# Attention, a dense layer and top-2 experts on one core: masks, maxima and weight norms computed by other engines, the order up to the first expert made anew, and the scatters of one expert left without an order

## The chip, the cores and the metric

The kernel runs on one core of one Trainium2 chip. A core has TensorE (PE, with its weight loads shown apart as PEld), VectorE (DVE), ScalarE (ACT), GpSimd (POOL) and SyncE (SP, which only issues transfers), and 16 DMA engines. The metric is the device time of one execution in microseconds, median of 3 runs.

## The reference

Three stages follow one another on 2304 tokens (4 batches of 576) of 512 values:

```python
# attention, 8 heads of 64, scale 1/8, twice
out_d     = sm_attn(mean4(q), mean4(k), mean4(v))          # 144 groups of 4 positions, repeated 4 times
scores    = where(|pos_i - pos_j| < 4, scale * q @ k.T, -1e9)
x         = repeat(out_d, 4) + softmax(scores) @ v
# dense layer, 512 -> 2048 -> 512
x         = relu(x @ w_in)**2 @ w_out
# 8 experts, 512 -> 1024 -> 512, each token goes to its best two
noisy     = x @ w_gate + log1p(exp(x @ w_noise)) * noise
top2, wts = best two of noisy, softmax over them
out[tok] += wts[tok, k] * (relu(x[tok] @ w1[e]) @ w2[e])   # for e in 0..7, k in 0..1
```

`w_in` and `w_out` come as 64-bit floats; the kernel turns their bits into 32-bit floats on the chip.

## The kernel before

**How it is tiled.** A float32 operand of a large product is scaled by a power of two and split into a high and a low float16 half (`wih`, `wil`; `gh`, `gl`), and each product is three float16 matmuls. The power of two comes from a norm, so nothing of `w_in` can be split before all of `w_in` has been read and converted. Attention is cut into 32 units (4 batches, 4 pairs of heads, 2 parts of the sequence). The dense layer goes over 9 chunks of 256 tokens, each in 8 steps of 256 hidden columns. The experts follow one after another, 5 tiles of 128 slots (the last of 112) each.

**What sets the order.** Up to the end of expert 0 the program is a list of tokens, `ORDER`, written out ahead: each token is one small function with an index, and each engine runs its instructions in the order of that list. Attention of unit u is `S` (local scores, L263), `D` (pooled scores, L277), `ml`/`md` (maxima, L286 to L299), `el`/`ed` (exponentials, ACT), `nl`/`nd` (sums and division, the division of batch 0 by POOL), `PT` (transposes and their evictions), `PW` (product with v) and `xb` (split of the result). `vg`, `vm`, `vs` load v, square it for its maximum, and sum groups of four. `Xa`, `Xb` make the scale of a batch. A piece of `w_in` goes through `il ia ib ic ij` (load; ACT, DVE, ACT, DVE convert it), `is` (ACT squares it, L960) and `in` (PE sums the squares of columns, L966); then `wS` makes the scale and `wh`/`wl` split the weights (ACT L982, DVE L989). `w_out` goes through `ol oa oB oc oj`, `os` (ACT squares and sums, L1011), `of` (scale), `oh`/`oo` (split). `M` is the first product of the dense layer (L577), `r` its activation (L585, L589, and the float16 copy `gh` by DVE, L599), `yh`/`yl` and `Y` the second product (L643, L619). Tokens from `ga` on are the gate and the rows written out for the experts; `pe`, `cm`, `cw` prepare and run expert 0.

**The start.** POOL builds the identity, a triangle and the masks with `affine_select` (L123 to L144); the mask scratch shares a buffer (`tag="jv"`) with the squares of v. DVE clears the buffers `pTs` and `vws`. The maximum over partitions is `partition_all_reduce` on POOL (L213 for x, L975 for `w_in`).

**The experts 1 to 7** are a plain loop (L1133). Turn e first calls `load_rows(e + 1)`: two transfers on SP and then four small DVE instructions, which make the row weights `om` and the row numbers `tk` (L857 to L862). Then come 16 steps of `c_m1` (12 matmuls, L873, then ACT L875 and DVE L876) between which the next expert's weights are split, then `load_e`, then 5 steps of `c_m2` (24 matmuls L887, DVE scales the result into `ob`, L889, POOL starts a scatter with addition to `out`, L890). Both `tk` and `om` have two buffers, `ob` has three. All scatters write the tensor `out`, so each waits until the one before it has landed.

Of the kernel before, what the change touches and what calls it, by code (L numbers as in the profile page):

```python
# [62 lines left out]
yh18 oo7 vw7 xb5 PW6 yh13 yh21 SD0 yl11 el8 pz0 yh26 yl21 el7 yh27 nl8 yl16 D9 S10 qk7 nl7 vg5 yh1 r6 yl25 yl19
yl8 yl29 nd7 r4 vm5 yl1 yl3 M7 G6 yl27 yl10 r7 yh16 yh30 yh20 xb6 PT7 yh8 D10 yl22 vs5 nd8 yh6 yh29 yh7 PW7 yh23
md9 pg0 yh31 ml9 yh28 PT8 yl20 yh25 ml10 el9 xb7 vw8 yh14 yl24 pf0 pf1 yl14 nl9 yl12 yl23 md10 vg6 ed9 M9 vm6
pf2 vs6 S11 PW8 r9 G7 yl18 pf3 nd9 vw9 M10 vw10 ed10 M13 yh24 D11 vg7 ip0 r10 el10 PT9 yl2 M12 vm7 md11 yh15 yl7
yl28 nl10 ml11 vs7 el11 nd10 yl31 ed11 Xa1 S13 r13 Xb1 pf4 pf5 xb8 vg8 D13 PT10 S12 D12 pf6 md13 M8 nl11 yl26
nd11 ed13 ml12 yl6 md12 yh19 PW9 vw11 r12 pf7 el12 PT11 yl30 zo0 ml13 xb9 yh4 r8 nl12 M11 PW10 r11 ed12 el13 M15
xb10 yh22 S14 nd12 S15 yl4 nl13 PW11 r15 xb11 M14 yl15 yh12 nd13 r14 PT12 D14 md14 ga1 M16 ml14 gb1 vm8 PT13
el14 ed14 D15 ga0 qk8 nl14 ml15 M17 el15 Y8 vw12 Y9 ip1 vs8 Y10 Y11 S16 qk9 nd14 gb0 md15 r16 vw13 r17 PW12 gc0  # L70
M19 ed15 G8 xb12 vg9 nl15 PW13 S17 gd0 nd15 Y12 PT14 vm9 Y13 ml16 gc1 gf0 gd1 M18 PT15 Y14 gf1 qk10 vs9 ge0 r19
Y15 ge1 D16 md16 M23 G9 r18 M22 gg1 gg0 ed16 vg10 vw14 xb13 D17 el16 r23 PW14 r22 M21 ga2 vm10 nl16 S18 md17 ga3
# [19 lines left out]
r67 Z2 ge15 gg15 r71 M69 r69 pe12 M70 r70 Y67 Y68 pe13 Y69 Y70 Y71 pe14 Z3 pe15 ga16 Z4 Z5 gb16 Z6 pe16 Z7 ga17  # L92
lr0 gc16 gb17 cm6 gd16 gc17 le1 gf16 gd17 cm7 pe17 ge16 pe18 gf17 gg16 cm0 cm3 cm1 pe19 pe20 ge17 pe21 gg17 cm2
cm4 pe22 cm5 pe23 pe24 cw1 pe25 pe26 pe27 cw0 lr1 pe28 cw2 cm15 pe29 cm10 cm9 pe30 cm11 cm8 pe31 cm14 pe32 cm13
cm12 pe33 lr2 le2 cw4 cw3
"""


@with_exitstack
def moe_kernel(ctx, tc, qk_in, vwin, vgrp, w_in, w_out, w_gate, w_noise, noise, w1, w2, out):  # L100
# [45 lines left out]
    for t in pms:  # L146
        nc.gpsimd.memset(t, 0.0)
# [1115 lines left out]
```

## Time and profile before

| | us |
|---|---|
| median of 3 runs (lowest, highest) | 1012.27 (1011.76, 1012.81) |
| the profiled execution, own time | 1015.63 |
| its span, first to last instruction | 1013.6 |
| PE, DVE, ACT, POOL busy | 921.0, 602.1, 484.9, 131.4 |
| mean granted clock of TensorE | 0.977 of full speed |

Busy times are those of the profiled execution and are a share of its span; a time left idle on PE is the span less 921.0, or 92.6 us. Rows of the trace give the start of an instruction or of a merged run of like instructions, its length, the engine, the source line, what it writes and reads, and in square brackets how long the engine had been idle and what it had waited for.

### The profile page before, as it was taken

What the parts mean: (1) busy time and instruction counts of PE and PEld (TensorE: products, weight loads), DVE (VectorE), ACT (ScalarE), POOL (GpSimd) and SP (SyncE); (2) the same over time, 40 slices, a digit from 0 to 9 for tenths busy, and PEclk for the clock granted to TensorE, in tenths of its full rate; (3) what the DMA queues carried; (4) which work ended last, traced back from release to release, by engine and by line L of the source; (5) the groups of instructions that cost most, each with busy time, mean ns of one, the idle gap of its engine ahead of it and who ended that gap; (6) DMA issues with size and microseconds to landing.
All of it is one profiled execution on the core that took longest, in us unless ns stands there. A gap on an engine that the chain in (4) does not pass through costs nothing. (4 is left out here: it accounts for less than half of the span.)

```text
span 1013.6 us, 20138 instructions
## 1 busy us (share of the span) xinstructions
PE 921.0 (91%) x8159; PEld 614.6 (61%) x8159; DVE 602.1 (59%) x1833; ACT 484.9 (48%) x1043; POOL 131.4 (13%) x171
## 2 busy tenths in 40 slices
PE   2538999999999999999999998999999899989992
PEld 1426888666676667666666464656565647455651
DVE  5899977678868776857677562525161616153220
ACT  4899956445544345343544544627162525341100
POOL 2312000010101000101011111020201020111111
PEclk9999899999999999999999898999999899999997
DMA  9743588533333111116124577637365463721212
GB/s 317 251 160 108 162 306 306 143 118 54 73 91 109 45 38 54 51 30 220 22 64 112 198 172 192 186 41 215 53 186 74 113 145 103 157 29 21 31 22 33
DMA packets 104184, 121.70 MB, mean 120 GB/s; under 512 B 69264, under 2 KB 69264, under 8 KB 102032
## 3 DMA queue, kind: packets, MB, share of 16 engines
q1 hardware_dynamic: 95568, 100.57, 34.1%
q0 software_dynamic: 8512, 19.74, 10.2%
q8 instruction: 66, 1.08, 0.4%
q14 instruction: 38, 0.31, 0.1%
HBM read 70.33 MB, written 35.28 MB: 104 GB/s over the span
## 5 line engine op out<-in xcount | busy, mean ns | idle before, releaser
L577 PE MATMUL ph<-xall,wih 128*128 128x256 f16 x1152 | 197.6, 278 | 3.9 <-ACT wih L982 3.8
L873 PEld LDWEIGHTS <-we 128*128 128x128 f16 x1536 | 153.3, 100 | 71.2 <-issue 20.9
L887 PE MATMUL po<-we,h 128*128 128x512 f16 (+1 forms) x840 | 182.4, 379 | 0.0
L873 PE MATMUL phc<-xT,we 128*128 128x384 f16 (+1 forms) x1152 | 158.2, 300 | 9.7 <-DVE h L876 9.7
L577 PE MATMUL ph<-xall,wil 128*128 128x256 f16 x576 | 159.6, 277 | 2.7 <-DVE wil L989 2.6
L887 PEld LDWEIGHTS <-h 128*128 128x128 f16 (+1 forms) x840 | 87.6, 104 | 92.3
L875 ACT ACTIVATE h<-phc 128x384 f16<-128x384 f32 (+1 forms) x112 | 47.6, 428 | 179.5 <-PE phc L873 161.6
L619 PE MATMUL y<-wo,gh 128*128 128x512 f16 x448 | 133.3, 379 | 0.0
L577 PEld LDWEIGHTS <-wih 128*128 128x128 f16 x1152 | 111.9, 100 | 22.1 <-ACT wih L982 3.9
L889 DVE TENSOR_SCALAR ob<-po,om 128x512 f32<-128x512 f32 (+1 forms) x35 | 26.3, 751 | 148.8 <-PE po L887 148.8
L890 POOL DMA_INDIRECT out_dram<-ob,tk x35 | 53.8, 1538 | 326.9 <-DVE ob L889 203.3
L619 PE MATMUL y<-wo,gl 128*128 128x512 f16 x224 | 84.9, 379 | 0.0
L876 DVE SCALAR_TENSOR_TENSOR h<-phc,h 128x384 f16<-128x384 f32 (+1 forms) x112 | 52.2, 479 | 50.2 <-ACT h L875 49.4
L780 POOL DMA_INDIRECT xs<-row,si x36 | 36.9, 1026 | 338.5 <-issue 133.5
L619 PEld LDWEIGHTS <-gh 128*128 128x128 f16 x448 | 42.1, 98 | 44.7 <-issue 0.4
L577 PEld LDWEIGHTS <-wil 128*128 128x128 f16 x576 | 57.3, 100 | 10.9 <-DVE wil L989 3.1
L585 ACT ACTIVATE r<-ph 128x512 f32<-128x512 f32 x72 | 42.3, 587 | 19.8 <-PE ph L577 19.0
L589 ACT ACTIVATE g<-r 128x512 f32<-128x512 f32 x72 | 45.4, 630 | 2.3
L602 DVE TENSOR_TENSOR gl<-g,gh 128x512 f16<-128x512 f32 x64 | 44.5, 696 | 2.3
L825 ACT ACTIVATE we<-w1raw,sce 128x1024 f16<-128x1024 f32 x32 | 35.2, 1139 | 18.5 <-DVE sce L158 15.2
L599 DVE CAST gh<-g 128x512 f16<-128x512 f32 x64 | 27.1, 423 | 26.2 <-ACT g L589 25.3
L826 DVE SCALAR_TENSOR_TENSOR we<-w1raw,sce,we 128x1024 f16<-128x1024 f32 x32 | 40.4, 1282 | 2.2 <-ACT we L825 1.8
(331 smaller groups left out, 1360.3 us busy)
## 6 DMA issues: line engine op xcount, KB each, us to landing
w1raw<-in_moe_w_dram SPq DMA_DIRECT2D x8, 2048.0 KB
w2raw<-in_moe_w_dram SPq DMA_DIRECT2D x8, 2048.0 KB
xs<-zrow SPq DMA_DIRECT2D x8, 1290.0 KB
qkT<-in_qk_dram SPq DMA_DIRECT2D x16, 579.0 KB
raw<-in_moe_w_out_dram SPq DMA_DIRECT2D x8, 1024.0 KB
out_dram<-zrow SPq DMA_DIRECT2D x1, 4864.0 KB
raw<-in_moe_w_in_dram SPq DMA_DIRECT2D x4, 1024.0 KB
vw<-in_vwin_dram SPq DMA_DIRECT2D x48, 76.0 KB
```

What stands on the lines that cost most here:

```text
L577: nc.tensor.matmul(ph[:, f], a[:, kk, fo], bb[:, kk], start=(n == 0), stop=(n == 11))
L585: nc.scalar.activation(r, ph, AF.Relu, scale=KAPPA)
L589: nc.scalar.activation(g, r, AF.Square)
L602: nc.vector.tensor_tensor(gl, g, gh, op=OP.subtract)
L619: nc.tensor.matmul(py[c, tt], a[:, o], bb[:, ft], start=(ft == 0 and n == 0), stop=(ft == 15 and n == 2))
L780: st = nc.gpsimd.indirect_dma_start(out=xs, out_offset=bass.IndirectOffsetOnAxis(ap=si[:, kk:kk + 1], axis=0), in_=roww, in_offset=None)
L826: nc.vector.scalar_tensor_tensor(wl[:, o], raws[i][:, o], ss[i], wh[:, o], op0=OP.mult, op1=OP.subtract)
L873: nc.tensor.matmul(ph[:, :n], a[:, fo], xT[:, bb], start=(i == 0), stop=(i == 11))
L875: nc.scalar.activation(hh[:, f], ph[:, :n], AF.Relu)
L876: nc.vector.scalar_tensor_tensor(hl[:, f], ph[:, :n], 0.0, hh[:, f], op0=OP.max, op1=OP.subtract)
L887: nc.tensor.matmul(po, a[:, f, jo], bb[:, do], start=(i == 0), stop=(i == 23))
L890: nc.gpsimd.indirect_dma_start(out=out, out_offset=bass.IndirectOffsetOnAxis(ap=tk[:m], axis=0), in_=ob[:m], in_offset=None, compute_op=OP ...
```

## The change

- The identity and the masks are made by DVE with two small matmuls that turn a row of numbers into a column; POOL keeps two memsets and one `affine_select`, for the triangle. The mask scratch has a buffer of its own, and `idh` is made later. ACT runs one exponential of a column first.
- For the units of batch 0 and for part 0 of batch 1 (12 units of 32) one more matmul (`idb` with `masks`) puts the masks into PSUM ahead of the local scores, and the addition by DVE falls away.
- The maximum over partitions is a transpose by PE, a maximum by DVE on one partition, and a matmul that spreads it. A token `Xm`, or `wT` and `wU`, stands for each further step.
- The norm of `w_in`: per piece 8 products of a 128x128 block of its upper 16 bits with itself, collected in four PSUM tiles (`in`), and per half two maxima by DVE (`is`, now two tokens and not eight). The squares by ACT and L966 fall away. The norm of `w_out`: 8 such products and one DVE instruction per piece (`os`), and the squares by ACT (L1011) fall away.
- `r` becomes `ra` in 56 of its 72 steps: the float16 copy is made by ACT, as a second square, and not by DVE.
- In the expert loop the row weights of experts 2 to 7 are made by `row_weights(e)` after the 16 steps of `c_m1` of the same expert. The scatters of one expert are declared independent of each other, except those of expert 0.
- `ORDER` is a new list of the same length.

```diff
 ORDER = """
...
-xb2 PW3 is6 oa1 in4 G4 oB1 in5 S7 in6 is7 ol3 oc0 ol2 in7 ed5 wS0 xb3 qk5 nl5 oc1 wh6 wh7 oj0 wl6 wh0 nd5 vw4 S8
-oa3 oa2 oj1 wh5 wl7 vw5 wh3 wl0 os1 oB2 M0 wl3 wh2 wl5 oB3 oc2 M5 oj2 wl2 os0 oc3 of1 oj3 wh1 wh4 os2 wl4 PW4 D7
...
+ib6 in2 in3 ic5 ml5 ia7 nl4 is3 PW2 ic6 el5 in4 ib7 ij5 vw3 xb2 ij6 ic7 oa3 ed5 in5 ij7 in6 in7 oB3 oa0 oB0 oa2
+is7 nd4 ol1 PW3 wS0 S6 oB2 oc0 oc3 wT0 oj3 oa1 wU0 oc2 vw4 oB1 os3 wh5 oj2 wh1 qk4 S7 wl5 xb3 oc1 vg5 D6 wh4 md6
+PT4 wl1 oj1 os2 wh0 oj0 wh7 wl0 nl5 vw5 wh6 M5 wl6 os1 wh2 wh3 qk5 wl7 M0 D7 wl4 qk6 of3 nd5 wl3 os0 wl2 ed6 r0
...
 """
...
-    idf = const.tile([P, P], F32, name="idf")
-    nc.gpsimd.memset(idf, 0.0)
-    nc.gpsimd.affine_select(idf, idf, [[-1, P]], OP.not_equal, 1.0, base=0, channel_multiplier=1)
...
-    masks = const.tile([P, 9, KW], BF16, name="masks")
-    mask = sp.tile([P, 512], BF16, tag="jv", name="mask", bufs=1)[:, :KW]
-    nc.gpsimd.memset(mask, 0.0)
-    for j in range(4):
-        m = mask[32 * j:32 * j + 32]
-        nc.gpsimd.affine_select(m, m, [[1, KW]], OP.is_ge, NEG, base=0, channel_multiplier=-1)
-        nc.gpsimd.affine_select(m, m, [[-1, KW]], OP.is_ge, NEG, base=6, channel_multiplier=1)
...
     pms = [ap.tile([P, 5, 64], F32, name=f"pm{i}", bufs=1) for i in range(2)]
-    for t in pms:
-        nc.gpsimd.memset(t, 0.0)
...
+    nc.gpsimd.memset(onesf, 1.0)
+    nc.gpsimd.memset(pms[0], 0.0)
+
+    pw = pms[1].rearrange("p a b -> p (a b)")
+    it, r32, dc = pw[:, :P], pw[:, P:2 * P], pw[:, 2 * P:2 * P + KW]
+    nc.vector.memset(it[:, 0:1], 0.0)
+    for n in (1, 2, 4, 8, 16):
+        nc.vector.tensor_scalar(it[:, n:2 * n], it[:, :n], float(n), None, op0=OP.add)
+    nc.vector.tensor_copy(r32.rearrange("p (a b) -> p a b", b=32), it[:, None, :32].to_broadcast([P, 4, 32]))
+    for n in (32, 64):
+        nc.vector.tensor_scalar(it[:, n:2 * n], it[:, :n], float(n), None, op0=OP.add)
...
+    nc.tensor.matmul(pc0_[:, 1:2], r32[0:1], onesf[0:1, 0:1], start=True, stop=True)
+    nc.tensor.matmul(pc0_[:, 0:1], it[0:1], onesf[0:1, 0:1], start=True, stop=True)
+    nc.vector.tensor_copy(pidx, pc0_[:, :2])
+    nc.vector.tensor_scalar(dc, it[:, :KW], pidx[:, 1:2], 3.0, op0=OP.subtract, op1=OP.subtract)
+    nc.vector.tensor_tensor(dc, dc, dc, op=OP.mult)
+    nc.vector.tensor_scalar(mask, dc, 9.5, NEG, op0=OP.is_gt, op1=OP.mult)
+    nc.vector.tensor_copy(masks, mask[:, None, :].to_broadcast([P, 9, KW]))
+    for j in (0, 64):
+        nc.vector.memset(masks[j:j + 32, 0, :3], NEG)
+        nc.vector.memset(masks[j + 32:j + 64, 7, KW - 3:], NEG)
+    nc.vector.tensor_scalar(idb, it, pidx[:, 0:1], None, op0=OP.is_equal)
+    nc.vector.tensor_scalar(idf, it, pidx[:, 0:1], None, op0=OP.is_equal)
+    nc.vector.memset(pms[1], 0.0)
     for i in range(2):
         nc.vector.memset(pTs[i][0], 0.0)
         nc.vector.memset(vws[i][32:64], 0.0)
+    nc.vector.tensor_copy(onesb, onesf)
+    nc.gpsimd.affine_select(trib, onesb, [[1, P]], OP.is_gt, 0.0, base=0, channel_multiplier=-1)
+
+    tiny = sp.tile([P, 1], F32, name="tiny", bufs=1)
+    nc.scalar.activation(tiny, onesf[:, :1], AF.Exp)
...
+    XB, GX, MB = 5, 3, 3
...
     def x_scale(b):
         m1 = sp.tile([P, 1], F32, tag="xm", name="xm")
         nc.vector.tensor_reduce(m1, vmx[b], AX.X, OP.max)
+        nc.vector.tensor_scalar(m1, m1, 1.0e-30, None, op0=OP.max)
+        sx[b] = across(m1)
+
+    def across(m1):
+
+        pt = psT.tile([P, 512], F32, tag="tp", name="pmx")
+        nc.tensor.transpose(pt[0:1, :P], m1, idf)
+        return pt
+
+    def across2(pt):
         m2 = sp.tile([P, 1], F32, tag="xm2", name="xm2")
-        nc.vector.tensor_scalar(m1, m1, 1.0e-30, None, op0=OP.max)
-        nc.gpsimd.partition_all_reduce(m2, m1, P, bass.bass_isa.ReduceOp.max)
-        sx[b] = m2
+        nc.vector.tensor_reduce(m2[0:1], pt[0:1, :P], AX.X, OP.max)
+        nc.tensor.matmul(pt[:, P:P + 1], onesf[0:1], m2[0:1], start=True, stop=True)
+
+    def x_scale1(b):
+        across2(sx[b])
 
     def x_scale2(b):
-        m2 = sx[b]
+        pt = sx[b]
         sx[b] = const.tile([P, 1], F32, name=f"sx{b}")
-        pow2_of_sumsq(sx[b], m2, A_X)
+        pow2_of_sumsq(sx[b], pt[:, P:P + 1], A_X)
...
+        pre = 2 * b + part < MB
+        if pre:
+            nc.tensor.matmul(s_[:, :ng * KW], idb, masks[:, 4 * part:4 * part + ng].rearrange("q g c -> q (g c)"),
+                             start=True, stop=False)
...
-                                     qT[o, 32 * t:32 * t + 32], kT[o, 32 * t:32 * t + KW], start=True, stop=True)
+                                     qT[o, 32 * t:32 * t + 32], kT[o, 32 * t:32 * t + KW], start=not pre,
+                                     stop=not pre or i == ng - 1)
...
-        nc.vector.tensor_tensor(pl, s_[:, :ng * KW].rearrange("q (g c) -> q g c", c=KW),
-                                masks[:, 4 * part:4 * part + ng], op=OP.add)
...
+        src = s_[:, :ng * KW].rearrange("q (g c) -> q g c", c=KW)
+        if 2 * b + part >= MB:
+            nc.vector.tensor_tensor(pl, src, masks[:, 4 * part:4 * part + ng], op=OP.add)
+            src = pl
+        nc.vector.tensor_reduce(mx[:, :ng], src, AX.X, OP.max)
...
+        R[e, j0, "mt"] = mt
+        if e < 2:
+            row_weights(e, j0, j1, pool)
+
+    def row_weights(e, j0, j1, pool):
+        n = j1 - j0
+        nb = 1 if pool is sp else 2
+        m = R[e, j0, "mt"].bitcast(F32)
...
-        nc.gpsimd.indirect_dma_start(
+        st = nc.gpsimd.indirect_dma_start(
             out=out, out_offset=bass.IndirectOffsetOnAxis(ap=tk[:m], axis=0), in_=ob[:m], in_offset=None,
             compute_op=OP.add)
+        prior = osc.setdefault(e, [])
+        for o in prior if e else ():
+            tc.declare_no_dep(st.ins, o.ins, reason="an expert's tokens are distinct, and what its empty slots add is 0")
...
-        pn = ps1.tile([P, 64], F32, tag="m1", name="pn")
+        pn = [ps1.tile([P, 512], F32, tag="m1", name=f"pn{i}") for i in range(2)]
+        pn += [ps2.tile([P, 512], F32, tag="m2", name=f"pm{i}") for i in range(2)]
+        top = sp.tile([P, 4], F32, name="top", bufs=1)
+        fresh = set(range(4))
+        done_ = [0] * 4
...
-            r.append(lambda: nc.scalar.activation(st["junk"], vi[:, kk, o], AF.Square))
-            r.append(lambda: norm(kk, c, st["junk"]))
+            r += [lambda: gram(kk, c), lambda: peak(c)]
             return r
 
...
+        def gram(kk, c):
+
+            v = vi.bitcast(BF16)[:, kk, 2048 * c:2048 * c + 2048].rearrange("p (f n w) -> p f n w", n=P, w=2)[:, :, :, 1]
             for f in range(8):
-                nc.tensor.matmul(pn[:, 16 * kk + 8 * c + f:16 * kk + 8 * c + f + 1], sq[:, P * f:P * f + P],
-                                 onesb[:, :1], start=True, stop=True)
+                i = 2 * c + f // 4
+                done_[i] += 1
+                nc.tensor.matmul(pn[i][:, P * (f % 4):P * (f % 4) + P], v[:, f], v[:, f], start=i in fresh,
+                                 stop=done_[i] == 16)
+                fresh.discard(i)
+
+        def peak(c):
+            for i in (2 * c, 2 * c + 1):
+                nc.vector.tensor_reduce(top[:, i:i + 1], pn[i], AX.X, OP.max)
 
         def scale():
...
-            n2 = sp.tile([P, 1], F32, tag="n2w", name="n2w")
-            nc.gpsimd.partition_all_reduce(n2, cm_, P, bass.bass_isa.ReduceOp.max)
-            pow2_of_sumsq(s_in, n2, A_WIN)
+            nc.vector.tensor_reduce(cm_, top, AX.X, OP.max)
+            W["mx"] = across(cm_)
+
+        def scale1():
+            across2(W["mx"])
+
+        def scale2():
+            pow2_of_sumsq(s_in, W["mx"][:, P:P + 1], A_WIN)
...
-                nc.scalar.activation(st_["raw"][:, :, 0].bitcast(F32), st_["v"], AF.Square, accum_out=acc[q_][:, c:c + 1])
+                w = st_["hi"]
+                pq = psT.tile([P, 512], F32, tag="tp", name="pq")
+                for k in range(8):
+                    nc.tensor.matmul(pq[:, :P], w[:, P * k:P * k + P], w[:, P * k:P * k + P], start=(k == 0), stop=(k == 7))
+                nc.vector.scalar_tensor_tensor(pq[:, P:2 * P], pq[:, :P], 1.0, idf, op0=OP.mult, op1=OP.mult,
+                                               accum_out=acc[q_][:, c:c + 1])
...
-    for k_, nm in enumerate(("il", "ia", "ib", "ic", "ij", "is", "in")):
+    for k_, nm in enumerate(("il", "ia", "ib", "ic", "ij", "in", "is")):
...
+        if e > 1:
+            row_weights(e, 0, NR, cp)
```

## Rows read from the trace of the kernel before

**Rows 1.** Windows from:to, length, busy us of PE PEld DVE ACT POOL, granted clock, DMA:
```profile
0.00:17.00 17.00, 0.80 (x34) 0.65 (x35) 5.30 (x12) 3.68 (x5) 4.50 (x25) 1.00 0.90 302
17.00:77.00 60.00, 27.12 (x514) 19.99 (x515) 53.88 (x97) 51.98 (x100) 15.20 (x21) 1.00 0.63 222
77.00:124.00 47.00, 41.30 (x464) 34.80 (x464) 44.52 (x72) 45.92 (x77) 5.21 (x4) 0.89 0.43 139
124.00:184.00 60.00, 59.26 (x947) 52.14 (x946) 45.14 (x137) 37.29 (x110) 3.01 (x9) 1.00 0.86 303
184.00:600.00 416.00, 409.88 (x3918) 274.40 (x3916) 303.17 (x1224) 194.38 (x494) 46.62 (x76) 0.99 0.33 86
```

**Rows 2.** Timeline of the first 77 us, some rows of DVE, POOL and PE:
```profile
5.26 1.35 DVE L240 TENSOR_REDUCE qkT<-qkT 128x288 f32<-128x1152 f32 x1 [1.14 <-DMA qkT<-in_qk_dram]
12.02 0.28 POOL L123 TENSOR_SCALAR_AFFINE_SELECT idf<-idf 128x128 f32<-128x128 f32 x1 [10.89 <-issue]
16.56 0.32 DVE L286 TENSOR_TENSOR pm<-S,masks 128x152 f32<-128x152 f32 x1 [0.83 <-POOL masks L142]
38.46 0.38 POOL L213 PARTITION_ALL_REDUCE xm<-xm  x1 [6.06 <-issue]
38.87 0.15 DVE L157 TENSOR_SCALAR es<-xm 128x1 int32<-128x1 int32 x1 [3.39 <-POOL xm L213]
76.92 0.39 PE L577 MATMUL ph<-xall,wil 128*128 128x256 f16 x1 [2.58 <-DVE wil L989]
```

**Rows 3.** Waits, 600 us to the end: us in total, times, longest:
```profile
DVE tk L862 <- DMA out_dram<-ob,tk: 35.0, 4, 10.8
PE phc L873 <- DVE h L876: 11.8, 5, 4.5
```

**Rows 4.** Chain that ended last, in order of time: start, us, what:
```profile
671.98 9.75 PE phc L873 x60
...
697.78 5.19 PE po L887 x24
...
750.69 25.90 PE po L887 x120
776.59 1.96 PE phc L873 x12
...
809.07 5.19 PE po L887 x24
...
861.72 5.19 PE po L887 x24
...
918.60 25.90 PE po L887 x120
```

**Rows 5.** Timeline of the last expert's second product, some rows of DVE and POOL:
```profile
975.16 0.75 DVE L889 TENSOR_SCALAR ob<-po,om 128x512 f32<-128x512 f32 x1 [4.37 <-PE po L887]
976.18 1.55 POOL L890 DMA_INDIRECT out_dram<-ob,tk  x1 [27.85 <-DVE ob L889]
...
995.88 0.75 DVE L889 TENSOR_SCALAR ob<-po,om 112x512 f32<-112x512 f32 x1 [4.43 <-PE po L887]
...
998.56 1.48 POOL L890 DMA_INDIRECT out_dram<-ob,tk  x1 [4.19 <-DMA out_dram<-ob,tk]
```

**Rows 6.** Groups by line and form, DVE and ACT: busy us, mean ns | idle:
```profile
L286 DVE TENSOR_TENSOR pm<-S,masks 128x152 f32<-128x152 f32 x7 | 2.2, 311 | 1.0 <-POOL masks L142 0.8 <-PE S L263 0.2
L298 DVE TENSOR_REDUCE nb<-S 128x2 f32<-128x288 f32 x4 | 1.8, 450 | 0.0
L960 ACT ACTIVATE raw<-vi 128x1024 bf16<-128x1024 f32 x4 | 4.2, 1052 | 0.0
L508 DVE SCALAR_TENSOR_TENSOR raw<-raw 128x1024 int32<-128x1024 int32 x8 | 9.6, 1213 | 0.0
L599 DVE CAST gh<-g 128x512 f16<-128x512 f32 x64 | 27.1, 423 | 26.2 <-ACT g L589 25.3
```

**Rows 7.** Timeline of PE, one 128x128x128 product at the higher clock:
```profile
95.84 0.22 PE L643 MATMUL y<-wo,gh 128*128 128x128 f16 x1
```

More of the change, by code (lines that the diff above doesn't have):

```diff
@@ L63 @@
[L63 to L72, printed above, removed]
@@ L484, in load32 @@
                 take()
-                st["v"] = dst if dst is not None else st["raw"].rearrange("p n w -> p (n w)")[:, n:].bitcast(F32)
+                st["v"] = dst if dst is not None else st["raw"][:, :, 1].bitcast(F32)
                 RQ[0].dma_start(st["v"], src)
@@ L579, in m1_mm, with g_tiles @@
         gt[c, fp] = ph
+    def g_tiles(c, fp):
+        if 0 < c < 6 and fp < GX:
+            gh = ap.tile([P, 512], F16, tag="gh", name="gh", bufs=GX)
+            gl = ap.tile([P, 512], F16, tag="gl", name="gl", bufs=GX)
+        elif c < NCH - 1:
+            gh = bp.tile([P, 512], F16, tag="gh", name="gh", bufs=8)
+            gl = bp.tile([P, 512], F16, tag="gl", name="gl", bufs=8)
+        else:
+            gh, gl = cw["g"][:, fp, 0], cw["g"][:, fp, 1]
+        return gh, gl
     def m1_ev(c, fp, act=True, cast=True):
@@ L589, in m1_ev @@
         nc.scalar.activation(g, r, AF.Square)
-        if 0 < c < 6 and fp < GX:
-            gh = ap.tile([P, 512], F16, tag="gh", name="gh", bufs=GX)
-            gl = ap.tile([P, 512], F16, tag="gl", name="gl", bufs=GX)
-        elif c < NCH - 1:
-            gh = bp.tile([P, 512], F16, tag="gh", name="gh", bufs=8)
-            gl = bp.tile([P, 512], F16, tag="gl", name="gl", bufs=8)
-        else:
-            gh, gl = cw["g"][:, fp, 0], cw["g"][:, fp, 1]
+        gh, gl = g_tiles(c, fp)
         if cast:
@@ L984, in hi, with lo @@
                 nc.vector.tensor_scalar(wih[:, :, o], vi[:, :, o], s_in, None, op0=OP.mult)
-        def lo(c):
+        def lo(c, eng=nc.vector):
             wih, wil = W["in"]
             o = slice(256 * c, 256 * c + 256)
-            nc.vector.scalar_tensor_tensor(wil[:, :, o], vi[:, :, o], s_in, wih[:, :, o], op0=OP.mult,
+            eng.scalar_tensor_tensor(wil[:, :, o], vi[:, :, o], s_in, wih[:, :, o], op0=OP.mult,
                                     op1=OP.subtract)
-        return [conv(kk, c) for kk in range(4) for c in range(2)], scale, hi, lo
+        return [conv(kk, c) for c in range(2) for kk in range(4)], (scale, scale1, scale2), hi, lo
     def wout_pieces():
@@ L1059, in moe_kernel @@
         "Xa": x_scale,
+        "Xm": x_scale1,
         "Xb": x_scale2,
```

117 lines of the change are left out of this document (60 added, 57 removed).

## The prediction, made before the change was run

> **What bounds the kernel now.** I read the windows by stage first [rows 1]. In each, PE's busy time is compared with the length. PE idles 16.2 us of the first 17 and 32.9 of the next 60. From 77 to 124 it idles 5.7, from 124 to 184 only 0.7, and from 184 to 600 6.1 of 416. So PE is the bound from about 77 us on, and before that something else is. From 17 to 77 DVE is busy 53.9 of 60 us and ACT 52.0: these two carry the conversion of w_in and attention of batch 0.
>
> The timeline of the start [rows 2] shows what holds them up. DVE is done with its first group sum at 6.6, then has no real work until the masks let it begin at 16.56. POOL stood 10.89 us ahead of its first `affine_select` with nothing to wait for. Later POOL stands 6.06 us ahead of the maximum over partitions, and DVE waits 3.39 us for it. The dense layer's products flow from 76.92, when `wil` is there.
>
> Then the waits of the last 400 us [rows 3] and the chain [rows 4]. DVE stands 35.0 us, in 4 waits, before it writes `tk`, until the scatters of the expert before last have landed. The `h` that PE needs is queued behind it, and PE waits 11.8 us in 5 places. The chain gives the length of each expert's first product between two second ones: expert 2 takes 697.78 - 671.98 = 25.80 us without such a wait. Expert 3 takes 750.69 - (697.78 + 25.90) = 27.01, expert 4 809.07 - 776.59 = 32.48, expert 5 861.72 - (809.07 + 25.90) = 26.75, expert 6 918.60 - (861.72 + 25.90) = 30.98.
>
> **The change part by part.**
>
> *Row weights later, scatters without an order.* `tk` and `om` of expert e are now made after e's own 16 steps. Their buffers were last used by expert e-2, whose scatters ended some 25 us before, so DVE no longer waits there. Queued behind them on DVE are only the scaling of `om` and the first `ob`, which needs the sums after 5.19 us of PE [rows 4]; four instructions on 128x5 values cost below 1 us and lie beside that. Their transfers stay where they were on SP. On POOL nothing stands behind a scatter but the next one. Experts 3 to 6 then take what expert 2 takes, with the same splitting of weights beside it: 27.01 + 32.48 + 26.75 + 30.98 - 4 x 25.80 = 14.0 us. This holds the idle time and what the clock lost behind it. I bound it from 12 to 14: a wait for the weights themselves could be next, but expert 2 shows none. The fifth wait of [rows 3] belongs to expert 1, behind expert 0, whose scatters keep their order; it stays.
>
> *The tail.* The last `ob` ends at 996.63, its scatter starts at 998.56, behind the one before. The first one of that expert started 0.27 after its `ob` ended [rows 5]. So the end comes 1.93 - 0.27 = 1.7 us sooner.
>
> *The start.* DVE's list ahead of the first `ml` is now some 23 small instructions, two matmuls in between, and the old clears. Before, all that DVE did in 17 us was 5.3 us [rows 1], 1.35 of it the group sum [rows 2]: the clears are at most 3.9, I take 2.4. The small ones I put at 0.15 to 0.3 each, from the 0.15 of a 128x1 one and the 0.32 of a 128x152 one [rows 2]: 3.5 to 7, taken as 5. With a begin at 1 us and 1.35 for the group sum, `ml` starts at 1 + 5 + 2.4 + 1.35 = 9.8, between 8 and 12, and not at 16.56.
>
> *DVE up to the first product.* Before: 53.4 us of work counted from the list, which the window's 53.88 bears out, in 60.4 us of time. In the new list, ahead of the first `wl` with its `wh`: 6 mask additions go, 4 at 0.31 and 2 at 0.35 (-1.9) [rows 6]; 4 maxima over 512 columns come, 0.6 each by extending the 0.45 for 288 (+2.4); the steps of the scale cost about the same. Moved behind: three `wl` (the wait of [rows 2] shows that the first product needs one), unit 6, one group sum, parts of unit 5 and two conversions (-10.8 in all); moved ahead: four conversions at 1.21 [rows 6], a group sum of v, one `wl` and small ones (+8.3). That is 53.4 - 2.5 = 50.9. ACT loses 8 squares at 1.05 [rows 6] and so is no longer as full as DVE. Of the 60.4 - 53.4 = 7 us that DVE lost before, 3.4 were the wait for POOL; the new maximum has its own hand-overs, so I keep 6. First product at 9.8 + 50.9 + 6 = 66.7, between 63 and 72, that is 10.2 us sooner than 76.92.
>
> POOL keeps one `affine_select`. The row shows 10.89 us of nothing ahead of the first one; if that begins only when DVE has written the ones, at 8.4, POOL is free at 19.3 and its division for unit 0 is 6 us late. The first `PW` lies 20 us of DVE's work into the list, so I charge nothing, and up to 3 us in the range. [...]
>
> *PE's added work.* Before the first product PE idles anyway: the products of w_in (64), the masks of batch 0 and most small maxima lie there. Behind it come 7 of the 8 pieces of w_out, 56 products of 128 columns. A product of 512 columns takes 25.90 / 120 = 0.216 us in a stream [rows 4], so 128 take 0.054: 3.0 us. If nothing overlapped, it would be the 0.22 of a single one [rows 7]: 12.3. Their operands are read with gaps, for which no row stands; I take the lower end since the shape is that of the streamed ones. Masks of batch 1 and three further maxima add about 1 us. Together 4.0, bounds 3 and 13.
>
> *Slack behind the first product.* Between 77 and 184 PE idles 6.4 us, and the clock of 0.89 over 47 us costs 5.2 [rows 1]. ACT no longer squares w_out, and the masks cost DVE less, so activations arrive sooner. I take 4.4 of these 11.6, bounds 0 and 11.6.
>
> *Casts.* 56 copies at 0.42 [rows 6] leave DVE and become squares on ACT, below 1.05 each. From 184 to 600 ACT is busy 194 of 416 us [rows 1], so they lie beside PE: nothing, with 3 either way.
>
> *Sum.* 10.2 - 4.0 + 4.4 = 10.6 at the front, 14.0 in the experts, 1.7 at the tail: 26.3. The profiled execution took 1015.63 us, so 989.3 by its own time; it stands 3.4 above the median of 1012.27, from which the same sum gives 986.
>
> **The rivals.**
> - *The front gives nothing.* The first product comes later than 66.7, or PE's new work costs its upper end. For it: DVE and ACT are both nearly full [rows 1], so any wait between them shows. Against: both have less to do. Only 14.0 + 1.7 is left: 1012.3 - 15.7 = 997.
> - *The front gives all.* PE is fed without gaps and stays at the higher clock: 10.2 - 3.0 + 11.6 = 19, and 3 more at expert 1: 974.
> - *The experts keep their wait.* Scatters in flight together slow each other so that `ob`, with three buffers, comes late, or the wait moves to another buffer. For it: scatters beside large loads take longer than others. Against: a buffer comes round only after three second products, 15.6 us. Left: 10.6 + 1.7, so 1000.
> - *Slower: PE's queue stands behind DVE.* PE now hands a result to DVE and takes one back for 8 norms of w_out, two steps of w_in and 8 of the batches' maxima: 18 places, all in two PSUM buffers that transposes and `PW` also use. PE runs in order, so each wait stops the dense layer. At the 2.58 us that PE waited for DVE in [rows 2], 18 of them cost 46 us: 1012.3 - 26.3 + 46 = 1032. It decides from 26.3 / 18 = 1.5 us each. Against: PE waits only 6.4 us in all from 77 to 184, where such hand-overs already abound, and the new list spreads each in two or three tokens with other work between.
>
> **How the numbers follow.** Forecast 0.56, front nothing 0.21, front all 0.12, experts keep their wait 0.06, slower 0.05. The first four are faster. About 0.2% is what a measurement of this kernel can tell from no change. Between the last two cases lie values near no change, 0.02 in all. So faster 0.93, same 0.02, slower 0.05. The range reaches from 974, the front's best case, to 1001, the front with nothing and the upper price of PE's new work in part; left out is the slower case and what lies beyond these ends.
>
> **What would show it.** Right: the first `ml` near 10 us and the first product near 67; no maximum over partitions on POOL; DVE's row of `tk` without a wait for a scatter, and PE's of `phc` with one wait left; first products of experts 2 to 6 all near 25.8 us; scatters starting 0.3 us after their `ob`. Wrong: waits of PE for DVE at the norms of w_out or at the maxima, products of 128 columns at 0.1 us or more in a stream, a clock below 0.89 from 67 to 124, or `ob` waiting for a scatter.

## The result and the profile after

The changed kernel took 999.26 us (median of 4 runs, 998.80 to 1000.35), the kernel before 1012.41 on the same chip: a ratio of 0.9872 (95% interval 0.9855 to 0.9889), so 13.1 us less. 986.0 was forecast, 26.3 less. On other chips before took 1012 to 1016 us, so the experiments below are compared by their ratio to before on the same chip. One more run of the changed kernel gave 0.983 (0.9795 to 0.9864).

The windows of the changed kernel, which answer to [rows 1] (from:to, length, busy us of PE PEld DVE ACT POOL, granted clock, DMA):

```profile
0.00:17.00 17.00, 5.28 (x111) 3.55 (x111) 11.69 (x44) 8.03 (x18) 1.21 (x10) 1.00 0.90 308
17.00:77.00 60.00, 34.61 (x450) 26.92 (x451) 49.98 (x87) 46.06 (x83) 17.37 (x18) 0.64 0.70 239
77.00:124.00 47.00, 45.76 (x615) 40.86 (x614) 42.09 (x84) 37.51 (x68) 8.02 (x6) 0.99 0.36 124
124.00:184.00 60.00, 57.40 (x909) 49.43 (x907) 43.18 (x129) 36.42 (x108) 0.99 (x6) 0.97 0.78 279
184.00:600.00 416.00, 408.37 (x3878) 273.11 (x3877) 284.47 (x1176) 219.67 (x543) 45.28 (x73) 0.99 0.36 92
```

From 77 to 124 PE idles 1.2 us and not 5.7, at a clock of 0.99 and not 0.89. But from 124 to 184 it idles 2.6 and not 0.7, and from 184 to 600 7.6 and not 6.1.

Waits of the changed kernel from 600 us on (us, times, longest), against [rows 3], and its chain, against [rows 4]:

```profile
DVE tk L906 <- DMA out_dram<-ob,tk: 10.6, 4, 2.7
PE phc L917 <- DVE h L920: 1.9, 1, 1.9
```

```profile
647.00 25.90 PE po L933 x120
672.90 9.75 PE phc L917 x60
...
698.70 25.90 PE po L933 x120
724.60 9.75 PE phc L917 x60
...
905.50 25.90 PE po L933 x120
931.40 25.44 PE phc L917 x192
956.84 25.91 PE po L933 x120
```

Two more pieces of the chain of before, the second products of expert 1 and of the last expert:

```profile
646.08 25.90 PE po L887 x120
...
969.94 10.37 PE po L887 x48
```

Every first product of experts 2 to 6 takes 25.80 us (698.70 - 672.90, and so on), as forecast, and the chain is PE alone. From expert 1's second product (646.08) to the end of the span the kernel before took 1013.6 - 646.08 = 367.5, now 997.4 - 647.00 = 350.4. That is 17.1 us less. And the second product of expert 1 itself starts 0.9 us *later* than before. The whole front, forecast at 10.6, brought nothing.

### The profile page after: what moved, and what is told of

It reads as the page before. It is cut to its first block, busy times and chain, and to the rows that moved or that the text cites. A ratio compares the mean times of both kernels' runs of the same rounds, so it can differ in the third digit from the quotient of the medians.

```text
span 997.4 us, 20288 instructions
## 1 busy us (share of the span) xinstructions
PE 928.7 (93%) x8254; PEld 624.9 (63%) x8254; DVE 580.4 (58%) x1809; ACT 497.4 (50%) x1076; POOL 131.4 (13%) x150
## 3 DMA queue, kind: packets, MB, share of 16 engines
q0 software_dynamic: 8512, 19.74, 10.4%
## 5 line engine op out<-in xcount | busy, mean ns | idle before, releaser
L917 PEld LDWEIGHTS <-we 128*128 128x128 f16 x1536 | 150.4, 98 | 56.4 <-issue 3.4
L917 PE MATMUL phc<-xT,we 128*128 128x384 f16 (+1 forms) x1152 | 154.4, 296 | 0.0
L935 DVE TENSOR_SCALAR ob<-po,om 128x512 f32<-128x512 f32 (+1 forms) x35 | 26.3, 751 | 147.0 <-PE po L933 147.0
L863 DVE SCALAR_TENSOR_TENSOR we<-w2raw,sce,we 128x1024 f16<-128x1024 f32 x32 | 40.5, 1274 | 1.2 <-ACT we L862 1.2
L656 PEld LDWEIGHTS <-gl 128*128 128x128 f16 x224 | 22.0, 98 | 26.9 <-issue 0.8
```

What stands on the lines that cost most here:

```text
L656: nc.tensor.matmul(py[c, tt], a[:, o], bb[:, ft], start=(ft == 0 and n == 0), stop=(ft == 15 and n == 2))
L863: nc.vector.scalar_tensor_tensor(wl[:, o], raws[i][:, o], ss[i], wh[:, o], op0=OP.mult, op1=OP.subtract)
L917: nc.tensor.matmul(ph[:, :n], a[:, fo], xT[:, bb], start=(i == 0), stop=(i == 11))
```

## The experiments

**1. The experts' two parts without the new front.** On the kernel before, the row weights moved and the scatters without an order:

```diff
         if e + 2 < E:
             load_e(e + 2)
+        if e > 1:
+            row_weights(e, 0, NR, cp)
...
+        for o in prior if e else ():
+            tc.declare_no_dep(st.ins, o.ins, reason="...")
```

> The kernel before with only the two parts of the change that lie in the experts: the row weights of expert 2 and later made after that expert's 16 steps, and no order between the scatters of one expert. Theory: the stretch behind expert 1's second product got 17.1 us shorter (367.5 to 350.4) and does not lean on the new front, which brought nothing; so 1012.4 - 17.1 = 995.3 us, and faster than the changed kernel by some 4. Rival: the front did gain, and the experts gain that much only behind it; then 1000 us or more here.

Measured: 995.73 us, ratio 0.9835 (0.9819 to 0.9852), 16.5 us less. The changed kernel's two runs gave 0.9872 and 0.983, so this part of its changes does at least as well as the whole; the intervals overlap with that of the second.

**2. The front without them**: the same two edits taken out of the changed kernel.

> The changed kernel with the experts as before (row weights early, scatters in order): the front alone. Theory: 999.3 + 17.1 = 1016.4 us, so no gain of the new front, some 4 us slower than before, DVE again waiting some 35 us before the tk rows. Rival (the front did bring 10): about 1002 us.

Measured: 1012.03 us, ratio 1.0004 (0.999 to 1.0018). The front alone is worth nothing; the loss of 4 that I expected isn't there either. In this run expert 1's second product starts at 643.51, in the second run of the changed kernel at 645.56, so the front lies between 2.6 ahead of before and 0.9 behind. One profile can't tell it more closely: kernels with the front of before start that product at 643.0 (experiment 1), 644.5 and 647.4 (experiment 3) by their timelines of PE.

**3. Each expert part alone.** First the row weights, with the scatters' order kept:

> The kernel before with the late row weights only; the scatters keep their order. Theory of the forecast: VectorE's wait before the tk rows goes and with it 14 us; the order of the scatters costs only the end, 1.7: 1012.2 - 14 = 998. Rival (with the scatters still one behind another, the first one of an expert waits for the last one of the expert before, and the buffers of ob come late): 1003 or more.

Measured: ratio 1.001 (0.9994 to 1.0025). The rival, and by more than it said: nothing at all. DVE's timeline of this run, some rows behind expert 2's last `ob`:

```profile
725.23 0.75 DVE L896 TENSOR_SCALAR ob<-po,om 112x512 f32<-112x512 f32 x1 [4.43 <-PE po L894]
726.01 0.24 DVE L864 SCALAR_TENSOR_TENSOR om<-mt 128x5 f32<-128x5 f32 x2
...
735.51 0.17 DVE L869 CAST tk<-mt 128x5 int32<-128x5 f32 x1 [7.26 <-DMA out_dram<-ob,tk]
```

The call stands later in the program, but DVE's own list has `om` and `tk` where they were: behind the fifth `ob` of the expert before last. The order of these lists is made when the kernel is built, and a later line in the program didn't move them. So `tk` waits as before, 35.8 us in 4 waits. Now the scatters, with the row weights where they were:

> The kernel before with one part alone: no order between the scatters of one expert; the row weights are made where they were. Theory, from the run with the late row weights alone (1.001 of before, VectorE still waits 35.8 us ahead of the tk rows): the whole gain of the experts is this part, 0.983 to 0.984 of before, VectorE's waits ahead of tk down to 10 or 11 us in 4. Rival (both parts are needed together): 0.99 or more.

Measured: ratio 0.9822 (0.9799 to 0.9845): the whole gain. The same place in the changed kernel:

```profile
724.64 0.75 DVE L935 TENSOR_SCALAR ob<-po,om 112x512 f32<-112x512 f32 x1 [4.43 <-PE po L933]
725.42 0.24 DVE L901 SCALAR_TENSOR_TENSOR om<-mt 128x5 f32<-128x5 f32 x2
...
730.38 0.17 DVE L906 CAST tk<-mt 128x5 int32<-128x5 f32 x1 [2.72 <-DMA out_dram<-ob,tk]
```

`tk` still waits for the last scatter, but that one starts 0.27 us behind its `ob` instead of behind four others: 2.7 us each time, 10.6 in four, while PE has 9.75 us of first products to go on with.

**4. The masks alone** on the kernel before, with its own order of tokens (`masks`, `idf` as in the change, the additions left on DVE).

> The kernel before with only the masks and identity made by VectorE and TensorE; mask additions and the order of the tokens as before. Theory of the forecast (VectorE's work sets the time of the first product): the first mask addition near 11 and not 16.6, first product of the dense layer near 71.5, time 1007. Rival (transfers set it): first px product at 30 to 31 as before, first product 75 to 77, time 1011 to 1013.

Measured: 1008.06 us, ratio 0.9952 (0.9933 to 0.9971), 4.2 us less. The first product with `wil` comes at 73.46 and not 76.92. The first mask addition starts at 10.02 and not 16.56; of these 6.5 us 3.5 arrive, and `px` waits 2.4 for the windows of unit 0 on the way. The theory for the most part. **Both together**, masks and experts, old order:

> The kernel before with its own order of tokens, with the masks by VectorE and TensorE, the late row weights and the scatters without an order. Theory: the two gains add up, 1012.2 - 4.2 - 16.5 = 991.5 us, 8 less than the changed kernel. Rival (the gain of the start is given back in the stretch up to the experts, as in the changed kernel): 995 to 996.

Measured: ratio 0.977 (0.975 to 0.9789), so they add up. Then once more, beside the changed kernel on one chip:

> The base of the two runs above once more, on the same chip: 0.977 of before again, 10 us less than the changed kernel.

> The changed kernel once more, beside the others on one chip: 0.987 of before again.

Measured: 990.60 (988.76 to 991.09) against 995.64 us (995.25 to 998.39), ratios 0.9775 (0.9742 to 0.9808) and 0.983. The rest of the change, the larger part of its text, costs 5 us.

**5. Where the start hangs.** The changed kernel's PE and SP (some rows of their timelines; SPq is SyncE issuing transfers):

```profile
28.07 0.45 PE L418 MATMUL px<-pTd,vd 72*64 72x64 f32 x8
35.45 1.13 PE L426 MATMUL px<-pT,vw 102*64 102x64 f32 x16 [6.92 <-DMA vw<-in_vwin_dram]
...
74.08 0.42 PE L610 MATMUL ph<-xall,wil 128*128 128x256 f16 x1
```

```profile
9.89 1.87 SPq L523 DMA_DIRECT2D raw<-in_moe_w_in_dram  x2
12.72 6.34 SPq L255 DMA_DIRECT2D vw<-in_vwin_dram  x4
19.61 4.58 SPq L523 DMA_DIRECT2D wil<-in_moe_w_in_dram  x2
```

PE, ACT and DVE stand for 6.9, 6.3 and 4.7 us between 28 and 37 because the windows of unit 0 (`vw`, two loads of 76 KB) land at 35. In the new order their loads stand behind the third and fourth load of w_in; in the old one those of unit 0 stood ahead of the fourth. So I moved both ahead (`vm3 ed1 vw0 vw1 il2` in place of `... il2 ... il3 ... vw1 ... vw0`):

> The changed kernel with one edit of its order: the loads of the values' windows of units 0 and 1 are issued ahead of the third and fourth load of w_in, not behind them. Theory: TensorE's 6.9 us wait for that transfer at 28.5 to 35.5 goes, the first px product comes near 29, the first product of the dense layer near 68 and not at 73.7, and the time falls by 3 to 6 us, to 993 to 996. Rival: the transfers are only swapped, the loads of w_in are late in their place and VectorE or ScalarE wait for them: first product 72 to 74, time 998 to 1000.

Measured: 999.07 us, ratio 0.9859 (0.9839 to 0.9879), first product at 75.47. The rival. `px` comes at 29, but now ACT waits for w_in:

```profile
10.79 6.30 SPq L255 DMA_DIRECT2D vw<-in_vwin_dram  x4
17.14 2.86 SPq L523 DMA_DIRECT2D raw<-in_moe_w_in_dram  x2
```

```profile
33.74 1.23 ACT L527 ACTIVATE raw<-raw,lob 128x1024 int32<-128x1024 uint32 x1 [6.77 <-DMA raw<-in_moe_w_in_dram]
```

Four loads of 76 KB hold SP for 6.3 us, 1.6 each. The loads of 1 MB beside them, with 13 times the bytes, hold it for 0.9 to 2.3 each, and one at 5.19 in the changed kernel for 0.33: here the hold went by the number of loads more than by their bytes. That transfers issued ahead of them fill a queue, as I took it below, is my reading of these rows; no view shows how full a queue is. What stands behind the four in SP's list is issued at 17 and not at 10. Is it the list, or the bytes? Three runs, the first with these loads left out (zeros stand in their place):

> The changed kernel with the loads of the values' windows of units 0 and 1 left out (zeros stand in their place). Theory (the wait for that transfer was the delay): the first px product near 29, the first product of the dense layer near 68 and not 73.7, 993 to 995 us on a chip where the changed kernel takes 999. Rival, which the run with these loads moved ahead speaks for (the transfers ahead of the start are too many in all, and without this wait the next w_in load is waited for): first product 72 or later, no more than 2 us gained.

Measured: first product at 68.19, ratio 0.9787 (0.9758 to 0.9816). That is the wait, and the 66.7 of the forecast is nearly there. Then only the one load ahead that stood ahead before:

> The changed kernel with the windows of unit 0 alone loaded ahead of the fourth load of w_in, as in the order of before, and those of unit 1 behind it. Theory (SyncE stands for 6.3 us while it issues the four window loads, because the transfers ahead of them fill the queue, and whatever is behind them in its list is late; so the fewest of them go ahead): the first px product near 29, the w_in loads late by 2 to 3 us instead of 7, first product of the dense layer at 69 to 71, 3 to 4 us less than the changed kernel, 0.980 of before. Rival (as in the run with both loads ahead, the wait only changes its place): first product 73 or later, 0.985.

Measured: first product at 73.80, ratio 0.9837 (0.981 to 0.9864): no gain that can be told from the changed kernel's two runs. Now units 2 and 3 wait for their windows, 3.4 and 3.5 us, where in the changed kernel only unit 3 did, for 2.7. And the same loads from GpSimd:

```diff
-            nc.sync.dma_start(vt[h0:h0 + KW, :n]...
+            (nc.gpsimd if (b, part) == (0, 0) and hp < 2 else nc.sync).dma_start(vt[h0:h0 + KW, :n]...
```

> The changed kernel with the windows of units 0 and 1 issued by GpSimd, ahead of its first division, and not by SyncE: they don't stand in SyncE's list, but the same bytes are moved. Theory (the place in SyncE's list is what costs, not the 0.3 MB): the loads of w_in are issued near 10 as in the changed kernel, first px product near 29, first product of the dense layer near 68, 4 to 6 us less, 0.978. Rival (the transfer engines are full from 4 to 30 us, so nothing is won by another queue): first product 72 or later.

```profile
10.07 1.90 SPq L523 DMA_DIRECT2D raw<-in_moe_w_in_dram  x2
12.88 1.86 SPq L523 DMA_DIRECT2D wil<-in_moe_w_in_dram  x2
```

```profile
18.23 2.34 POOL L255 DMA_DIRECT2D vw<-in_vwin_dram  x4
```

```profile
29.76 0.64 PE L426 MATMUL px<-pT,vw 102*64 102x64 f32 x16
...
69.11 0.42 PE L610 MATMUL ph<-xall,wil 128*128 128x256 f16 x1
```

Measured: first product at 69.11, ratio 0.9792 (0.9767 to 0.9816), which is 4 to 8 us less than the two runs of the changed kernel. The same bytes, issued 5.5 us later than the changed kernel issues them, land in time (9.5 us after their issue, `px` at 29.76 without a wait), and w_in isn't late: `wil` is issued at 12.88 and not 19.61. So it is the place in SyncE's list and not the amount. How the transfers of the two queues share the 16 engines, and on how many of them one load runs, no run here shows.

**6. The clock of the start.** In the changed kernel it stood mostly at the lower level (granted 0.50; in windows of 2 us 0.80, 1.00 and 0.56 from 40 to 46) from 31 to 78, behind the gap at 28 to 35. Here PE is kept busy through that gap:

> The changed kernel with 46 products of 342 columns, whose result nobody reads, put ahead of the first px product, where TensorE stood 6.9 us: so it is busy from 28 to 35. If that idle time is what drops its clock to the lower level from 30 to 78, the clock stays at the higher one, the products of the start take half as long, the first product of the dense layer comes at 70 to 73 and the first 4.5 us of its stream take half: 995 to 997 us. Rival (the start is paced by transfers, VectorE and ScalarE, not by TensorE's clock): first product at 73 to 74, and 997 to 999 for the stream alone. If the clock falls nevertheless, nothing changes.

Windows of that run (columns as above):

```profile
28.00:36.00 8.00, 8.00 (x54) 5.12 (x51) 3.83 (x6) 2.09 (x4) 7.77 (x8) 1.00 0.95 285
36.00:44.00 8.00, 4.07 (x111) 3.47 (x111) 6.48 (x13) 7.05 (x16) 1.91 (x3) 0.98 0.74 267
44.00:52.00 8.00, 5.41 (x52) 4.31 (x52) 7.31 (x11) 6.43 (x10) 1.24 (x1) 0.50 1.00 367
```

Measured: first product at 74.35, ratio 0.9883 (0.9844 to 0.9922). The clock stayed up until 44 (1.00 and 0.98), and nothing came of it. From 44 to 68 it was low (0.50) all the same; what that costs this run can't tell.

**7. The norm of w_out.** Taken back to 8 squares on ACT in the changed kernel:

> The changed kernel with the norm of w_out taken as before, by 8 squares on ScalarE of 1.05 us, in the same places; the 64 small products on TensorE and the 8 reads of them by VectorE go. Theory (TensorE is the bound from the first product of the dense layer on, and a group of 8 of these products took 0.92 us of its stream): 6.7 us less on TensorE, 999.2 - 6.7 = 992.5 us. Rival 1 (each product costs what 128 columns of a streamed one cost, 0.054): 996.2. Rival 2 (ScalarE is late with the activations instead): 999 or more.

Measured: ratio 0.991 (0.9892 to 0.9929), slower than the changed kernel by 0.4 to 0.8%. Rival 2. The window of 77 to 124 us of this run, its first product with `wil`, and PE's longest waits from 72 to 124:

```profile
77.00:124.00 47.00, 38.90 (x500) 32.84 (x500) 38.63 (x66) 42.54 (x78) 5.84 (x4) 0.87 0.32 119
```

```profile
70.84 0.28 PE L610 MATMUL ph<-xall,wil 128*128 128x256 f16 x1 [0.93 <-DVE wil L1053]
```

```profile
PE ph L610 <- ACT r L629: 4.1, 2, 3.7
PE ph L610 <- ACT wih L1046: 3.0, 1, 3.0
```

The first product comes 3.2 us sooner, since no group of w_out stands ahead of it in PE's list, but then ACT is busy 42.5 of 47 us and late: from 77 on PE idles 8.1 us where it idled 1.2, at a clock of 0.87 and not 0.99. Put the other way into the old order (base: masks, experts):

> The old order of tokens, masks by VectorE and TensorE, late row weights and scatters without an order (the kernel that took 0.977 of before), and with it the norm of w_out by 64 products on TensorE in place of 8 squares on ScalarE. Theory: TensorE's stream is the bound behind the first product, and a group of 8 took 0.92 us in it: 6.7 us slower, 0.984. Rival: TensorE still idles 7.3 us between 72 and 124 here because ScalarE is full (21.9 of 24 us), so the squares that ScalarE loses pay for the products: within 2 us, 0.975 to 0.979.

Measured: 994.47 us, ratio 0.9802 (0.9764 to 0.9839), against 990.60 and 0.9775 for its base on the same chip: 3.9 us slower by the medians, intervals that overlap. Between theory and rival. The price of one product was read from the trace of one run, beside a group with operands that lie close, whose result nobody reads:

> The kernel with the norm of w_out by products in the old order (0.980 of before), and behind each group of 8 products, whose operands are read with a gap, a group of 8 of the same size whose operands lie close, with a result that nobody reads. Theory (the gap makes the difference, not the shape): a close group takes 0.4 to 0.5 us of TensorE's stream at the higher clock, a group with gaps 0.92. Rival (so short a product never runs at the pace of a stream): both 0.9.

```profile
107.14 1.12 PE L1040 MATMUL pq<-raw 128*128 128x128 bf16 x8
108.08 0.63 PE L1042 MATMUL pq<-onesb 128*128 128x128 bf16 x8
108.54 0.39 PE L656 MATMUL y<-wo,gh 128*128 128x128 f16 x4
108.76 1.11 PE L1040 MATMUL pq<-raw 128*128 128x128 bf16 x8
```

From start to start, a group of 8 with gaps takes 0.94 us (108.08 - 107.14), a close one 0.46 (108.54 - 108.08): 0.117 and 0.058 each. So it isn't the shape. The gap is the likely cause; the groups also differ in that the close one reads one tile of ones throughout, but the float16 products beside it, whose weights change, take 0.055 (0.22 for 4). These rows are at a granted clock of 1.00. At 0.50 (66 to 72 us) a group with gaps takes 0.93 as well, a close one 0.82: the clock didn't set the pace of the products with gaps.

**8. Casts and maxima**, each alone on the base of masks and experts. The casts (`r` to `ra` for the same 56):

> The same base (0.977 of before), with 56 of the 72 casts of the activations done by a second square on ScalarE and not by a copy on VectorE. Theory of the forecast: nothing, within 3 us, 0.974 to 0.980. Rival: the steps that TensorE waits for become longer (ScalarE's three passes of 0.6 us one behind another before VectorE can start), and TensorE's idle time from 184 to 600 grows from 6.5 us to 10 or more: 0.981 or more.

Measured: 990.50 us, ratio 0.9776 (0.9742 to 0.9811), base 990.60: nothing, as forecast. The maxima of the batches (`Xm` put in two to four tokens behind `Xa`):

> The kernel that took 0.977 of before (old order, masks by VectorE and TensorE, late row weights, scatters without an order), with the four maxima over partitions of the batches by a transposition, a reduction and a product in place of GpSimd's reduction. Theory: only the first of the four lies in a stretch where others wait for it (the 9.4 us of GpSimd and VectorE ahead of es), so 0.973 to 0.977. Rival (the two products and the wait of TensorE for VectorE's reduction between them cost TensorE more than it saves): 0.979 or more.

Measured: ratio 0.9853 (0.983 to 0.9876), base 0.977: 8 us slower. The rival. PE's waits of this run from 124 to 600:

```profile
PE pmx L229 <- DVE xm L223: 3.5, 3, 1.3
PE px L410 <- DVE es L169: 1.8, 1, 1.8
```

The first product with `wil` does come 1.3 to 1.7 us sooner (70.37), but PE's idle time from 124 to 600 is 11.7 us and not 6.7 to 7.2 as in the two runs of the base, 5.3 of it in these four waits. The granted clock adds to it: it was 0.97 from 124 to 184, 0.98 from 300 to 375 and 0.97 from 525 to 580 in this run, where the second run of the base had 1.00 in all three and the first one 0.99 from 450 to 600. The window times what the clock lacked is 1.8, 1.5 and 1.7 us here, and 1.5 in that run. Idle time and clock together, less what the first product gained, come to 6 to 9 us, which is about the 8. Other places in the list weren't tried.

## Why the forecast was wrong, and where it was right

**The experts** (14.0): the size was right, the reason wrong. From expert 1's second product to the last expert's, 323.9 us became 309.8 (969.94 - 646.08, 956.84 - 647.00): 14.0. The sum priced the lost time itself, so it comes out whatever removes the wait; with the reason that I gave, it came out by luck. I gave the 14.0 us to the moved row weights; experiment 3 shows that these did nothing and that the scatters' order was all of it. I had read "made after e's own 16 steps" off the program and not asked where DVE's list would have it, and the sign that I had named, `tk` without a wait for a scatter, did not come (10.6 us in 4). I had seen the scatters' order as a matter of the tail only, though [rows 3] names the scatter as what `tk` waits for. In the chain of before, expert 2's five were under way from 704.03 to 734.04, 30 us, where PE's second product takes 25.9.

**The tail** (1.7): the last `ob` to its scatter 0.27 us, as forecast. From the last expert's second product to the end it gained 3.1 (43.66 to 40.56). 1.65 of it is the term that I had; the other 1.45 lies behind the issue of the last scatter, and no run tells its cause.

**The first product** (10.2): 2.8. It came at 74.1, forecast 66.7, from 63 to 72. Two steps of the term failed. The first is the 6 us that I let DVE lose. The first maximum began at 10.85 (forecast 9.8), and from there to the end of the first `wil`, at 70.26, DVE was busy 48.8 us (50.9) and lost 10.65 (6). 6.8 of these were two waits that go back to `vw`. I took 6 from the waits of before and didn't follow the loads that the new order moves, past SyncE above all, though the column of the transfers in [rows 1] stands at 0.90 in the first 17 us. The rival's "any wait between them shows" was this one.

The second step is that `wil` would release the first product, as it did before:

```profile
68.99 1.27 DVE L1053 SCALAR_TENSOR_TENSOR wil<-vi,s_in,wih 128x1024 f16<-128x1024 f32 x1
```

```profile
72.75 1.10 PE L1078 MATMUL pq<-raw 128*128 128x128 bf16 x8 [1.66 <-ACT pt L393]
73.68 0.61 PE L610 MATMUL ph<-xall,wih 128*128 128x256 f16 x2
```

At 70.26 PE still had transposes and a group of products of w_out ahead of it in its list, and that group stood 1.66 us for ACT: 3.4 us more, up to 73.68, for which the sum had no term. Where the products of w_out were taken away (experiment 7), the first product with `wil` waited for `wil` again and came at 70.84. The runs without the wait for `vw` (68.19 and 69.11) still had that group ahead of it; both cures together weren't run.

**PE's added work** (4.0): six groups of 8 products of w_out lie behind the first product, 0.93 us each from start to start, 5.6 in all and not 48 x 0.054 = 2.6. With the 1 us that I took for masks and maxima, which no run shows alone, that makes 6.6. The step that failed is the choice of the lower end "since the shape is that of the streamed ones"; it lay in the range of 3 to 13, and 0.1 us or more in a stream was among my signs of being wrong. The operands lie 8 bytes apart, and such products ran at half the pace of close ones, 0.117 and 0.058 us (experiment 7).

**The slack behind it** (4.4): about 2. Between the first product and expert 1's second one PE idles 17.0 us, before 16.0, and what the clock lacks of full speed, in windows of 3 us, comes to 9.0 and not 11.9. It was won and lost again: up to 124 idle time and clock gain 7.5 us together, and behind it they lose 5.4. 2.8 for the start - 6.6 + 2.1 = -1.7, where the two profiles show -0.9; their fronts differ by more than that from run to run (experiment 2). The new order's waits of PE from 124 to 600:

```profile
PE pl L733 <- DMA yT<-row: 2.9, 2, 2.2
PE S L307 <- DVE pm L318: 2.6, 1, 2.6
PE S L307 <- DVE pm L321: 1.6, 1, 1.6
```

In the kernel before the first was 0.4 and the other two were not there. I hold the new order, which I had taken as given, for their cause; no run has it alone.

**The casts** (0): right, as tried in the old order (experiment 8).

**GpSimd's start** (0 to 3): nothing, more clearly than I thought: its `affine_select` ran at 4.51.

**The sum**: by the profiled spans -0.9 + 14.0 + 3.1 = 16.2 = 1013.6 - 997.4; the medians differ by 13.1, since the profiled run of before stood 3.4 above its median and that of after at its own. So it is the rival "the front gives nothing", 997, that came, by the first of the reasons it named: the first product came later than 66.7. PE's new work cost about twice what I took for w_out, but not its upper end. "The experts keep their wait" did not come. "PE's queue stands behind DVE" is not what cost the most, but PE's waits in its own list are real: the first product pays 3.4 us for what stands ahead of it there, 1.66 of it a wait for ACT, and the maxima in experiment 8 pay for waits behind DVE.

## What to carry to other kernels

Before pricing a wait away, ask what in the waiting engine's own list stands where, and what the awaited thing itself waits for: here five scatters one behind another were the length; lifting their order was worth 17 us, moving in the program the instructions that wait for them nothing. When an order by hand is made anew, follow each load past the queue that issues it: four loads of 76 KB held SyncE's list for 6.3 us, where those of 1 MB beside them took 0.9 to 2.3 each, and a second queue brought the first product forward by 5 us (74.08 to 69.11). Ask of the awaited product, too, what stands ahead of it in its own engine's list. And time a product with operands that have gaps (0.117 us here, 0.058 without) before moving work to TensorE; the version with only the masks and the experts' two parts beat the whole change by 5 us.

## What the runs showed of the chip that I had not expected

- A product of 128 columns whose bf16 operands lie 8 bytes apart took 0.117 us at a granted clock of 1.00 and 0.116 at 0.50, one with close operands 0.058 at 1.00. 4 bytes apart, as in the products of w_in, the gap cost nothing: 8 of them took 0.46 us in the run of experiment 6, from 37.30 to 37.76, at a clock of 0.98 (36 to 44).
- GpSimd's idle time of 10.9 us ahead of its first `affine_select` [rows 2] was not a price of that instruction. It is there in six runs that have the batches' maxima on GpSimd (10.4 to 11.3 us: before, and runs of experiments 1, 3, 4 and 7), ahead of the third instruction of the kernel's own there, an iota in the run with the masks alone; without them, in the changed kernel, its run of experiment 5 with GpSimd's loads and the maxima alone of experiment 8, it is gone. The start of GpSimd in that run:

```profile
0.94 0.36 POOL L134 MEMSET pm<- 128x320 f32 x1
11.98 0.14 POOL L474 IOTA trash<- 128x1 f32 x1 [10.68 <-issue]
```

and in the changed kernel:

```profile
1.36 0.13 POOL L494 IOTA trash<- 128x1 f32 x1
4.51 0.29 POOL L163 TENSOR_SCALAR_AFFINE_SELECT trib<-onesb 128x128 bf16<-128x128 bf16 x1 [3.02 <-DVE lob L500]
```

Why the reduction, which runs 20 us later, should cost at the start, no run tells.
- Lifting the scatters' order did not make them land later: of the 25 from 640 to 900 us, 4.8 us in the middle in the changed kernel (4.4 to 8.9), 4.7 before (4.4 to 11.0). But they start 5.18 us apart there, at the pitch of `ob` (704.94, 710.12, 715.30), so only the slowest ever overlapped the next one; what several in flight cost, no run shows.
